# A retention, expert and SoLU kernel on one core: decay table by transposes, last tile's rows turned by DRAM, last scaling on two engines

## The chip, the core and the metric

The kernel runs on one core of a Trainium2 chip. A core has a matrix engine (TensorE, PE here) that reads SBUF and writes PSUM, three engines for elementwise work (VectorE, DVE; ScalarE, ACT; GpSimd, POOL), a sync engine (SyncE, SP) that here issues most transfers, and DMA queues that move data between DRAM and SBUF. Each engine takes its instructions in the order of the program and waits on semaphores for the others. PEld is PE's loading of the stationary operand. The metric is the time of one execution on the device in microseconds; the median of three runs is given.

## What is computed

Three stages, each in float32, on 1536 tokens of 512 numbers (2 batches, 8 heads of 64, 768 steps):

```python
gamma = 1.0 - 2.0 ** (-5.0 - np.arange(H))          # one decay a head
for t in range(S):                                   # retention
    state = gamma * state + outer(k[:, :, t], v[:, :, t])
    y[:, :, t] = (1 / sqrt(D)) * q[:, :, t] @ state
# experts: the two best of 8 by noisy logits, softmax over the two
h = np.maximum(x[mask] @ w1[e], 0.0)
out[mask] += top2_w[mask, k, None] * (h @ w2[e])
# SoLU block: 512 -> 1024 -> 512
h = x @ w_in
solu = h * softmax(h)
ln = (solu - mean(solu)) / sqrt(var(solu) + 1e-6) * g_ln
return ln @ w_out
```

## The kernel before

**Stages.** The tokens are 12 tiles of 128 (`NT = 12`; tile i is chunk i // 2 of batch i % 2). First, attention runs tile by tile in chunks of 128 steps: scores by head (`scores`, L430), masked on DVE (L434), multiplied with the scaled values (`y_out`, L447), scaled by a decay table `decT` while they leave PSUM (L450), and a state per batch (`kv`, L458). Then the tokens of each expert are gathered from DRAM, and eight experts run two products each. Last, the 12 tiles go through the SoLU block. Most products are made of three: each operand is split into a high part (rounded by ACT) and the rest (subtracted by DVE), and high*high, high*low and low*high are added up, so one product of the last stage (`out_mm`, L959) is 24 instructions: 16 with the high part of the rows, then 8 with the low part.

**Order.** The order is the order of the code (`tc.manual_schedule()`): each engine gets its instructions as the functions are called, and tile pools with a few buffers each add the waits.

**The start.** `scale_v(0)` (DVE, L417), `scores(0)`, then `dec_t(0)`: for each of the 8 heads PE multiplies a column of the loaded decay, broadcast to 64 columns, with the identity (L302), which leaves the decay of each head along the free axis on 64 partitions. ACT copies that from PSUM (L304). `kv(0)`, `y_out(0)`, `scores(1)` follow. 34 small products (L269) stand ahead of all.

**The last stage.** The loop over i (L1226 to L1257) works on several tiles at once. In turn i it takes the rows of tile i that came back from DRAM (`z_parts`), scales and stores tile i - 1 (`store_out`), makes the scale of tile i + 1, and lets PE do the input product of tile i + 2 in two halves of 512 columns (`h_in`, 12 instructions each, L866), with the transposes of tile i + 3 between them (`x2_t`). Then come the row maximum (`solu_max`), exponential and normalization (`solu`) of tile i + 2, the turning of its rows, and PE's product of tile i.

**Turning rows.** The product needs the 1024 numbers of a token along partitions. `z_turn` (tiles 1 to 10) does it off PE: DVE transposes 32x32 blocks (L935), SP issues four writes to DRAM (L938) and one read back with the blocks in place (L940); two turns of the loop later `z_parts` rounds what came back to the high part on ACT (L948), and DVE subtracts (L950). `z_t` (tiles 0 and 11) does it with 8 transposes on PE (L920), from whose PSUM ACT and DVE make the two parts (L922, L925). The last tile's product is made in two halves of 256 columns, each scaled by ACT (L965) and stored; the last store is issued by ACT's own queue.

The launch is one program; the block behind `tc.If(full == 1)` does not run with these inputs. `out` is written by the stores of L966 alone.

Of the kernel before, what the change touches and what calls it, by code (L numbers as in the profile page):

```python
# [8 lines left out]
F32 = mybir.dt.float32  # L9
# [6 lines left out]
AF = mybir.ActivationFunctionType  # L16
# [28 lines left out]
def retnet_moe_solu(ctx, tc, qT, kT, k, v, w_gate, w_noise, noise, w1, w2, w_in, w_out, g_ln,  # L45
                    decay, out, dbg=None):
    nc = tc.nc
    B, NC, _, H, D = v.shape
    HP = H // 2
    S = NC * 128  # L50
    NT = B * NC
    E = w1.shape[0]
    DM = H * D
# [19 lines left out]
    def bank(tag, shape=(128, 512)):  # L73
        pool, n = psum[tag]
        return pool.tile(list(shape), F32, tag=tag, name=tag, bufs=n)
# [67 lines left out]
    def row0(i):  # L143
        c, b = order[i]
        return b * S + c * 128
# [145 lines left out]
    def dec_t(c):  # L291
        if c >= NC:
            return
        decT[c] = wk.tile([128, HP, 128], F32, tag="decT" if c else "decT0", name="decT", bufs=2 if c else 1)
        if c:
            for hp in range(HP):
                nc.scalar.activation(decT[c][:, hp], decT[0][:, hp], AF.Copy, scale=step[:, c, hp:hp + 1])
            return
        p = bank("c3", (128, HP, 128))
        for h in range(H):  # L300
            r = slice(h % 2 * 64, h % 2 * 64 + 64)
            nc.tensor.matmul(p[r, h // 2, :], dec[:, 1, c, h:h + 1].to_broadcast([128, D]), ident, start=True, stop=True,  # L302
                             skip_group_check=True)
        nc.scalar.activation(decT[c], p, AF.Copy)  # L304

    def dec_steps():
# [547 lines left out]
    def h_in(i, s):  # L854
        if i >= NT:
            return
        if s == 0:
            PH[i] = bank(f"d{i % 2}", (128, 2, 512))
        hi, lo = X2T[i]
        n = 0  # L860
        for d in range(KD):
            c = slice(d * 128, (d + 1) * 128)
            f = slice(s * 512, s * 512 + 512)
            wh, wl = unit_t[8 * E + d]
            for x, w in ((hi, wh), (hi, wl), (lo, wh)):
                nc.tensor.matmul(PH[i][:, s, :], x[:, c], w[:, 0, f], start=(n == 0), stop=(n == 3 * KD - 1))  # L866
                n += 1

    def row_max(pool, ph):
        t = pool.tile([128, 16], F32, tag="st", name="st", bufs=3)  # L870
        nc.vector.reduce_max(t[:, 0:1], ph, axis=AX.X)
        nc.vector.tensor_scalar_mul(t[:, 0:1], t[:, 0:1], -1.0)
        return t
# [27 lines left out]
    def solu_max(i):  # L901
        if i >= NT:
            return
        ST[i] = row_max(m2, PH[i].rearrange("p a f -> p (a f)"))
# [38 lines left out]
    def z_parts(i):  # L943
        hi = m2.tile([128, KF, 4, 32], F32R, tag="zh", name="zh")
        lo = m2.tile([128, KF, 4, 32], F32R, tag="zl", name="zl")
        t = ZD.pop(i).rearrange("p a k j -> p k a j")
        for k in (slice(0, KF // 2), slice(KF // 2, KF)) if i == 1 else (slice(0, KF),):
            nc.scalar.activation(hi[:, k], t[:, k], AF.Copy)  # L948
        ZT[i] = tuple(x.rearrange("p k a j -> p (k a j)") for x in (hi, lo))
        return lambda: nc.vector.tensor_sub(lo, t, hi)  # L950

    OUT = {}

    def out_mm(i, c=slice(0, DM)):
        hi, lo = ZT[i]
        p = bank("b")[:, c]
        terms = [(z, f, n) for z, ns in ((hi, (0, 1)), (lo, (0,))) for f in range(KF) for n in ns]
        for m, (z, f, n) in enumerate(terms):
            nc.tensor.matmul(p, z[:, f * 128:(f + 1) * 128], unit_t[8 * E + 4 + f // 2][n][:, f % 2, c],  # L959
                             start=(m == 0), stop=(m == len(terms) - 1))  # L960
        OUT[i] = p

    def store_out(i, c=slice(0, DM)):
        o = m2.tile([128, DM], F32, tag="o", name="o", bufs=3)
        nc.scalar.activation(o[:, c], OUT.pop(i), AF.Copy, scale=RS[i])  # L965
        (nc.scalar if c.stop == DM and c.start else nc.sync).dma_start(out[row0(i):row0(i) + 128, c], o[:, c])  # L966


    ep = ex_ctx.enter_context(tc.tile_pool(name="ep", bufs=1, reuse_waits="tile"))
# [253 lines left out]
    feed(n_units, n_units)  # L1223
    h_in(1, 1)

    for i in range(NT):  # L1226
        gather(i + 5)
        low = None
        if i == 0:
            z_t(0, lambda: solu_max(1))  # L1230
            solu(1)
            z_turn(1)
            RS[0] = RS[0]()
        else:
            if i < NT - 1:
                low = z_parts(i)
            store_out(i - 1)
        if i + 1 < NT:
            RS[i + 1] = RS[i + 1]()
        h_in(i + 2, 0)  # L1240
        if low:
            low()
        x2_t(i + 3)
        mix(i + 4)
        h_in(i + 2, 1)
        solu_max(i + 2)
        solu(i + 2)
        if i + 2 < NT - 1:
            z_turn(i + 2)
        if i == NT - 2:  # L1250
            z_t(i + 1)
        if i < NT - 1:
            out_mm(i)
        else:
            for c in (slice(0, DM // 2), slice(DM // 2, DM)):
                out_mm(i, c)
                store_out(i, c)  # L1257
# [135 lines left out]
```

## Time and profile before

| | |
|---|---|
| median of 3 runs | 514.53 us (514.43 to 514.7) |
| the profiled execution | 515.7 us, its span 513.9 us |
| PE busy | 506.6 us (99% of the span), 3068 instructions |
| PEld, weight loads | 463.9 us (90%) |
| DVE busy | 364.6 us (71%) |
| ACT busy | 233.2 us (45%) |
| POOL busy | 106.3 us (21%) |
| DMA | 111.92 MB, mean 218 GB/s |
| granted TensorE clock | 0.998 of full |

The span runs from the first to the last instruction of the profiled execution. Busy times of engines overlap each other. Times in rows are microseconds from the span's start, and a duration stands behind each start; "idle before" is the time that the engine stood before the row, with what released it. Rows of PE can overlap by a fraction of a microsecond, since products are pipelined; the chain of waits shows the same work without overlap.

### The profile page before, as it was taken

The page shows a single profiled execution, that of the slowest core. Times are in us where ns is not written, and L with a number is a line of the kernel's source. Part 1 is how long each engine was busy: PE and PEld are TensorE (multiplying, and loading weights), DVE is VectorE, ACT ScalarE, POOL GpSimd, SP SyncE. Part 2 cuts the span into 40 slices and gives each one's busy share as a digit, 9 for nine tenths or more (in the row PEclk, how much of TensorE's full clock was granted, in tenths as well). Part 3 has the DMA queues.
Part 4 walks back from the last instruction along what each step waited for, and adds up shares of the span by engine and source line. Part 5 has one row for each costly group of instructions (what it writes and reads, how often), then busy time and mean ns, then how long its engine had stood idle before and what let it go on. Part 6 is the DMA issues. An engine that isn't in the chain of part 4 may idle for free.

```text
span 513.9 us, 8633 instructions
## 1 busy us (share of the span) xinstructions
PE 506.6 (99%) x3068; PEld 463.9 (90%) x3068; DVE 364.6 (71%) x731; ACT 233.2 (45%) x440; POOL 106.3 (21%) x209
## 2 busy tenths in 40 slices
PE   9999999999999999999999999999999999999996
PEld 8898898989999999999999999998878888888885
DVE  4668778756876886877778778799277767666650
ACT  2578734443353443344435443545354644444431
POOL 4124100513002104004003000002244336311120
PEclk9999999999999999999999999999999999999999
DMA  8989531797978988979899968568553565643341
GB/s 259 347 319 368 208 103 42 243 348 266 328 225 230 294 248 203 352 199 283 296 239 324 288 200 237 198 172 222 160 190 106 166 184 149 206 134 103 102 123 47
DMA packets 71857, 111.92 MB, mean 218 GB/s; under 512 B 9760, under 2 KB 37152, under 8 KB 71808
## 3 DMA queue, kind: packets, MB, share of 16 engines
q1 hardware_dynamic: 65952, 96.54, 61.5%
q0 software_dynamic: 4368, 14.29, 8.9%
q10 hardware_dynamic: 1488, 0.48, 0.4%
q8 instruction: 26, 0.43, 0.4%
q14 instruction: 23, 0.19, 0.1%
HBM read 83.50 MB, written 27.79 MB: 217 GB/s over the span
## 4 chain that ended last, share of the span: by engine, by line
PE 90%; issue 5%; DMA 2%; DVE 2%; POOL 1%; ACT 0%; POOLq 0%; ACTq 0%; DVEq 0%
PE c L1077 23%; PE b L959 13%; PE b L729 12%; PE a L729 12%; PE d L866 11%; PE c L1200 3%; PE xr L480 3%; PE s L430 3%; PE c L447 2%; PE c L458 2%; PE c L443 2%; DMA xr<-xd,rows_r 2%; PE a L844 1%; PE c L269 1%; DVE wl L197 0%
## 5 line engine op out<-in xcount | busy, mean ns | idle before, releaser
L201 DVE TENSOR_TENSOR wl<-wr,wh 128x1024 fp32r<-128x1024 f32 x64 | 76.7, 1219 | 13.5 <-ACT wh L200 13.5
L1077 PE MATMUL c<-hh,wh 128*128 128x448 f32 (+5 forms) x224 | 79.1, 353 | 0.0
L1077 PE MATMUL c<-hl,wh 128*128 128x448 f32 (+5 forms) x224 | 78.9, 352 | 0.0
L1077 PE MATMUL c<-hh,wl 128*128 128x448 f32 (+5 forms) x224 | 78.8, 352 | 0.0
L200 ACT ACTIVATE wh<-wr 128x1024 fp32r<-128x1024 f32 x68 | 69.4, 1049 | 8.5 <-DMA wr<-in_moe_w_dram 8.5
L729 PE MATMUL b<-xh,wh 128*128 128x192 f32 (+8 forms) x144 | 47.2, 335 | 0.2 <-ACT xh L644 0.2
L729 PE MATMUL b<-xh,wl 128*128 128x192 f32 (+8 forms) x144 | 46.7, 332 | 0.0
L1077 PEld LDWEIGHTS c<-hh,wl 128*128 128x128 f32 x224 | 42.2, 188 | 1.3
L1077 PEld LDWEIGHTS c<-hh,wh 128*128 128x128 f32 x224 | 42.1, 188 | 1.3
L1077 PEld LDWEIGHTS c<-hl,wh 128*128 128x128 f32 x224 | 42.1, 188 | 1.3
L729 PE MATMUL a<-xh,wh 128*128 128x256 f32 (+7 forms) x128 | 43.1, 341 | 0.0
L729 PE MATMUL a<-xh,wl 128*128 128x256 f32 (+7 forms) x128 | 42.9, 339 | 0.0
L866 PE MATMUL d<-wh,x2h 128*128 128x512 f32 x96 | 38.8, 404 | 0.0
L959 PE MATMUL b<-wh,zh 128*128 128x512 f32 (+1 forms) x104 | 38.4, 375 | 0.0
L959 PE MATMUL b<-wl,zh 128*128 128x512 f32 (+1 forms) x104 | 38.4, 375 | 0.0
L866 PE MATMUL d<-wl,x2h 128*128 128x512 f32 x96 | 37.9, 395 | 0.0
L866 PE MATMUL d<-wh,x2l 128*128 128x512 f32 x96 | 37.8, 394 | 0.0
L1115 POOL COPY pace<-hh 1x1 f32<-1x1 f32 x20 | 9.7, 485 | 135.4 <-ACT hh L733 135.4
L733 ACT ACTIVATE hh<-b 128x192 fp32r<-128x192 f32 (+8 forms) x36 | 17.1, 475 | 43.6 <-PE b L729 40.9
L733 ACT ACTIVATE hh<-a 128x256 fp32r<-128x256 f32 (+7 forms) x32 | 15.9, 496 | 45.8 <-PE a L729 45.8
L1040 ACT ACTIVATE xh<-xt 128x428 fp32r<-128x428 f32 (+5 forms) x24 | 13.0, 540 | 45.1 <-DVE xt L1038 45.1
L1004 POOL DMA_INDIRECT xr<-xd,rows_r x27 | 28.1, 1040 | 25.4 <-DVE rows_r L677 15.9
(258 smaller groups left out, 1091.5 us busy)
## 6 DMA issues: line engine op xcount, KB each, us to landing
wr<-in_moe_w_dram SPq DMA_DIRECT2D x64, 512.0 KB
zd<-zs SPq DMA_DIRECT2D x40, 128.0 KB
zc<-zd SPq DMA_DIRECT2D x10, 512.0 KB
xs<-xr SPq DMA_DIRECT2D x18, 256.0 KB
raw<-in_moe_w_in_dram SPq DMA_DIRECT2D x8, 512.0 KB
raw<-in_moe_w_out_dram SPq DMA_DIRECT2D x8, 512.0 KB
xq<-xs SPq DMA_DIRECT2D x16, 208.0 KB
yg<-yr SPq DMA_DIRECT2D x16, 208.0 KB
```

The source lines that it names most:

```text
L200: nc.scalar.activation(hi, t, AF.Copy)
L201: (nc.gpsimd if u < LEAD else nc.vector).tensor_sub(lo, t, hi)
L430: nc.tensor.matmul(p[:, s, hp, :], KT[i][r, hp, :], QT[i][r, hp, :], start=True, stop=True)
L480: nc.tensor.matmul(t[:, d // 2, at:at + 128 + G2], XT[i][:, d, :], unit[d // 2][:, G2 - G2 * (d % 2):][:, :128 + G2], start=(d % 2 == 0), ...
L729: nc.tensor.matmul(p, w[:, 0, f * 128:(f + 1) * 128], x[:, d, c], start=(n == 0), stop=(n == len(terms) - 1))
L733: nc.scalar.activation(hh[:, f, c], p, AF.Relu)
L866: nc.tensor.matmul(PH[i][:, s, :], x[:, c], w[:, 0, f], start=(n == 0), stop=(n == 3 * KD - 1))
L959: nc.tensor.matmul(p, z[:, f * 128:(f + 1) * 128], unit_t[8 * E + 4 + f // 2][n][:, f % 2, c], start=(m == 0), stop=(m == len(terms) - 1))
L1004: nc.gpsimd.indirect_dma_start(out=t[b], out_offset=None, in_=xd[:], in_offset=bass.IndirectOffsetOnAxis(ap=rows_r[:, e - 1, b:b + 1], axi ...
L1040: nc.scalar.activation(hi, t, AF.Copy)
L1077: nc.tensor.matmul(py[d][:, :CAPS[e]], c, h[:, f, :CAPS[e]], start=(f == 0 and n == 0), stop=(f == KF - 1 and n == 2))
L1200: nc.tensor.matmul(py, h[:, f, c], w[:, f % 2], start=(f == 0 and n == 0), stop=(f == KF - 1 and n == 2))
```

## The change

Four things change in the code.

**The decay table.** `dec_t(0)` first lets DVE copy the eight columns, each spread over 64 columns, to a tile `wide` (128x512, in the ring of the `xT` tiles), and PE then transposes its four 128x128 blocks. ACT's copy from PSUM stays.

**The last tile's rows.** Tile 11 goes through `z_turn` and `z_parts` as the others do; ACT's rounding is in two halves there, as for tile 1. `z_t` is left for tile 0.

**A product begun inside another's place.** `out_mm` takes a part of its 24 instructions. In turn 8 PE does the first 12 of tile 8's product; the other 12 come in turn 9, behind the input product of tile 11. Tile 8 is scaled and stored after the exponential of tile 11. The small tiles `st` get a fourth buffer.

**The last scaling.** Of the last 256 columns DVE scales 128 and ACT 128.

```diff
--- before.py
+++ after.py
@@ -296,11 +296,12 @@
             for hp in range(HP):
                 nc.scalar.activation(decT[c][:, hp], decT[0][:, hp], AF.Copy, scale=step[:, c, hp:hp + 1])
             return
+        wide = wk.tile([128, HP, 128], F32, tag="xT", name="wide", bufs=3)
+        nc.vector.tensor_copy(wide.rearrange("p q (s d) -> p (q s) d", s=2),
+                              dec[:, 1, c, :, None].to_broadcast([128, H, D]))
         p = bank("c3", (128, HP, 128))
-        for h in range(H):
-            r = slice(h % 2 * 64, h % 2 * 64 + 64)
-            nc.tensor.matmul(p[r, h // 2, :], dec[:, 1, c, h:h + 1].to_broadcast([128, D]), ident, start=True, stop=True,
-                             skip_group_check=True)
+        for hp in range(HP):
+            nc.tensor.transpose(p[:, hp, :], wide[:, hp, :], ident)
         nc.scalar.activation(decT[c], p, AF.Copy)
 
     def dec_steps():
@@ -867,7 +868,7 @@
                 n += 1
 
     def row_max(pool, ph):
-        t = pool.tile([128, 16], F32, tag="st", name="st", bufs=3)
+        t = pool.tile([128, 16], F32, tag="st", name="st", bufs=4)
         nc.vector.reduce_max(t[:, 0:1], ph, axis=AX.X)
         nc.vector.tensor_scalar_mul(t[:, 0:1], t[:, 0:1], -1.0)
         return t
@@ -944,26 +945,33 @@
         hi = m2.tile([128, KF, 4, 32], F32R, tag="zh", name="zh")
         lo = m2.tile([128, KF, 4, 32], F32R, tag="zl", name="zl")
         t = ZD.pop(i).rearrange("p a k j -> p k a j")
-        for k in (slice(0, KF // 2), slice(KF // 2, KF)) if i == 1 else (slice(0, KF),):
+        for k in (slice(0, KF // 2), slice(KF // 2, KF)) if i in (1, NT - 1) else (slice(0, KF),):
             nc.scalar.activation(hi[:, k], t[:, k], AF.Copy)
         ZT[i] = tuple(x.rearrange("p k a j -> p (k a j)") for x in (hi, lo))
         return lambda: nc.vector.tensor_sub(lo, t, hi)
 
     OUT = {}
 
-    def out_mm(i, c=slice(0, DM)):
+    def out_mm(i, c=slice(0, DM), part=slice(0, 3 * KF)):
         hi, lo = ZT[i]
-        p = bank("b")[:, c]
+        if not part.start:
+            OUT[i] = bank("b")[:, c]
         terms = [(z, f, n) for z, ns in ((hi, (0, 1)), (lo, (0,))) for f in range(KF) for n in ns]
-        for m, (z, f, n) in enumerate(terms):
-            nc.tensor.matmul(p, z[:, f * 128:(f + 1) * 128], unit_t[8 * E + 4 + f // 2][n][:, f % 2, c],
+        for m, (z, f, n) in list(enumerate(terms))[part]:
+            nc.tensor.matmul(OUT[i], z[:, f * 128:(f + 1) * 128], unit_t[8 * E + 4 + f // 2][n][:, f % 2, c],
                              start=(m == 0), stop=(m == len(terms) - 1))
-        OUT[i] = p
 
     def store_out(i, c=slice(0, DM)):
         o = m2.tile([128, DM], F32, tag="o", name="o", bufs=3)
-        nc.scalar.activation(o[:, c], OUT.pop(i), AF.Copy, scale=RS[i])
-        (nc.scalar if c.stop == DM and c.start else nc.sync).dma_start(out[row0(i):row0(i) + 128, c], o[:, c])
+        p = OUT.pop(i)
+        if c.start and c.stop == DM:
+            m = (c.start + c.stop) // 2
+            nc.vector.tensor_scalar_mul(o[:, m:c.stop], p[:, m - c.start:], RS[i])
+            nc.scalar.activation(o[:, c.start:m], p[:, :m - c.start], AF.Copy, scale=RS[i])
+            nc.scalar.dma_start(out[row0(i):row0(i) + 128, c], o[:, c])
+        else:
+            nc.scalar.activation(o[:, c], p, AF.Copy, scale=RS[i])
+            nc.sync.dma_start(out[row0(i):row0(i) + 128, c], o[:, c])
 
 
     ep = ex_ctx.enter_context(tc.tile_pool(name="ep", bufs=1, reuse_waits="tile"))
@@ -1223,6 +1231,7 @@
     feed(n_units, n_units)
     h_in(1, 1)
 
+    HALF = 12
     for i in range(NT):
         gather(i + 5)
         low = None
@@ -1232,9 +1241,9 @@
             z_turn(1)
             RS[0] = RS[0]()
         else:
-            if i < NT - 1:
-                low = z_parts(i)
-            store_out(i - 1)
+            low = z_parts(i)
+            if i != NT - 3:
+                store_out(i - 1)
         if i + 1 < NT:
             RS[i + 1] = RS[i + 1]()
         h_in(i + 2, 0)
@@ -1243,13 +1252,17 @@
         x2_t(i + 3)
         mix(i + 4)
         h_in(i + 2, 1)
+        if i == NT - 3:
+            out_mm(i - 1, part=slice(HALF, 3 * KF))
         solu_max(i + 2)
         solu(i + 2)
-        if i + 2 < NT - 1:
+        if i == NT - 3:
+            store_out(i - 1)
+        if i + 2 < NT:
             z_turn(i + 2)
-        if i == NT - 2:
-            z_t(i + 1)
-        if i < NT - 1:
+        if i == NT - 4:
+            out_mm(i, part=slice(0, HALF))
+        elif i < NT - 1:
             out_mm(i)
         else:
             for c in (slice(0, DM // 2), slice(DM // 2, DM)):
```

On PE, the start before (`c_285` is the PSUM tile of the decay table, `unit_169` holds the identity):

```order
L430 MATMUL s<-qt,kt 128x128 x8
L302 MATMUL c_285<-unit_169,dec 64x128 x8
L458 MATMUL c_256<-vp,kn 128x128 x4
L447 MATMUL c_313<-pm,vp 64x128 x8
L430 MATMUL s<-qt,kt 128x128 x8
```

and on PE, the same place now:

```order
L431 MATMUL s<-qt,kt 128x128 x8
L304 MATMUL c_287<-unit_169,wide 128x128 x4
L459 MATMUL c_256<-vp,kn 128x128 x4
L448 MATMUL c_311<-pm,vp 64x128 x8
L431 MATMUL s<-qt,kt 128x128 x8
```

The eight products with the decay are replaced by four that read `wide`, at the same place between the first scores and the update of the state.

On DVE, the start now, where `wide` is made (before, the same rows stood there without the copy):

```order
L283 TENSOR_SCALAR causal<-jp 128x128
L285 TENSOR_SCALAR before<-jp 128x128
L418 TENSOR_TENSOR vp<-vt,dec 128x512
L435 TENSOR_TENSOR pm<-s,causal 128x512 x2
L300 COPY wide<-dec 128x512
L451 TENSOR_TENSOR xT<-c_311,decT 128x512
```

The copy stands behind the two masked scores, which read the PSUM tile `s` of the first scores.

On PE, near the end, before: the end of the input product of tile 11 (`d1_5382`) and what follows (`b_5419` is the product of tile 9):

```order
L866 MATMUL d1_5382<-wh_4184,x2h_5308 128x512
L866 MATMUL d1_5382<-wl_4185,x2h_5308 128x512
L866 MATMUL d1_5382<-wh_4184,x2l_5309 128x512
L959 MATMUL b_5419<-wh_4188,zh_5369 128x512
L959 MATMUL b_5419<-wl_4189,zh_5369 128x512
```

and on PE, the same place now (`d1_5365` is the input product of tile 11, `b_5342` the product of tile 8, `b_5426` that of tile 9):

```order
L867 MATMUL d1_5365<-wl_4183,x2h_5306 128x512
L867 MATMUL d1_5365<-wh_4182,x2l_5307 128x512
L961 MATMUL b_5342<-wh_4423,zh_5274 128x512
L961 MATMUL b_5342<-wl_4424,zh_5274 128x512
L961 MATMUL b_5342<-wh_4423,zh_5274 128x512
L961 MATMUL b_5342<-wl_4424,zh_5274 128x512
L961 MATMUL b_5342<-wh_4186,zl_5275 128x512 x2
L961 MATMUL b_5342<-wh_4194,zl_5275 128x512 x2
L961 MATMUL b_5342<-wh_4417,zl_5275 128x512 x2
L961 MATMUL b_5342<-wh_4423,zl_5275 128x512 x2
L961 MATMUL b_5426<-wh_4186,zh_5355 128x512
```

The second half of tile 8's product, 4 instructions with the high part and 8 with the low part, has moved behind the input product of tile 11 and ahead of tile 9's.

On ACT, the last rows before, with the semaphores that each waits for (`zh<-a` are the last tile's rows from PE's transposes):

```order
L879 ACTIVATE ee,st<-d_5382,st 128x1024 [waits DVE_49,PE_49,Activation_49]
L948 ACTIVATE zh<-zc 128x1024 [waits DMAHW5_49]
L965 ACTIVATE o<-b,st 128x512 [waits DMAHW2_49,PE_49,Pool_49]
L890 ACTIVATE ee,st<-z 128x1024 [waits DVE_49]
L922 ACTIVATE zh<-a 128x512 [waits PE_49] x2
L965 ACTIVATE o<-b,st 128x512 [waits DMAHW0_49,PE_49,Pool_49]
L965 ACTIVATE o<-b,st 128x256 [waits DMAHW6_49,PE_49,Pool_49]
L965 ACTIVATE o<-b,st 128x256 [waits DMAHW7_49,PE_49,Activation_49]
L966 DMA out_dram<-o 128x256 [waits DMAHW2_49,Activation_49]
```

and on ACT, the last rows now:

```order
L880 ACTIVATE ee,st<-d_5365,st 128x1024 [waits DVE_49,PE_49,Activation_49]
L973 ACTIVATE o<-b,st 128x512 [waits DMAHW4_49,PE_49,Pool_49]
L949 ACTIVATE zh<-zc 128x1024 [waits DMAHW5_49]
L973 ACTIVATE o<-b,st 128x512 [waits DMAHW2_49,PE_49,Pool_49]
L891 ACTIVATE ee,st<-z 128x1024 [waits DVE_49]
L949 ACTIVATE zh<-zc 128x512 [waits DMAHW3_49,Activation_49]
L949 ACTIVATE zh<-zc 128x512
L973 ACTIVATE o<-b,st 128x512 [waits DMAHW0_49,PE_49,Pool_49]
L973 ACTIVATE o<-b,st 128x256 [waits PE_49,DMAHW6_49,Activation_49,Pool_49]
L970 ACTIVATE o<-b,st 128x128 [waits DMAHW4_49,DVE_49,Activation_49]
L971 DMA out_dram<-o 128x256 [waits DMAHW7_49,Activation_49]
```

The scaling of tile 8 stands behind the exponential of tile 11, the last tile's rows come from DRAM (`zc`), and the last 128 columns wait for DVE in place of PE.

## Rows read from the trace of the kernel before

**Rows 1.** The page: busy time of each engine, its share, its instructions.

```profile
PE 506.6 (99%) x3068; PEld 463.9 (90%) x3068; DVE 364.6 (71%) x731; ACT 233.2 (45%) x440; POOL 106.3 (21%) x209
```

**Rows 2.** Waits of PE, longest that it has: us in total, times, longest.

```profile
PE a L1034 <- DMA xr<-xd,rows_r: 0.8, 1, 0.8
```

**Rows 3.** Chain of waits, the start: start us, us, engine, tile, line.

```profile
1.05 3.81 PE c L269 x34
4.86 1.81 PE s L430 x16
6.68 1.02 PE c L302 x16
7.70 1.09 PE c L458 x8
...
9.81 1.09 PE s L430 x16
```

**Rows 4.** Timeline of DVE, the start: start us, us, what [idle before].

```profile
6.73 1.29 DVE L434 TENSOR_TENSOR pm<-s,causal 128x512 f32<-128x512 f32 x2 [0.55 <-PE s L430]
...
9.93 0.69 DVE L450 TENSOR_TENSOR xT<-c,decT 128x512 f32<-128x512 f32 x1 [1.91 <-PE c L447]
```

**Rows 5.** Groups of DVE by form, 0 to 30 us: busy us, mean ns.

```profile
L367 DVE CAST col<-col 128x128 f16<-128x128 f32 x1 | 0.2, 221 | 0.0
```

**Rows 6.** Groups of DVE by form, 380 us to the end.

```profile
L950 DVE TENSOR_TENSOR zl<-zc,zh 128x1024 fp32r<-128x1024 f32 x10 | 12.0, 1195 | 2.9 <-ACT zh L948 2.9
L885 DVE TENSOR_SCALAR z<-ee,st 128x1024 f32<-128x1024 f32 x12 | 9.8, 813 | 0.4
```

**Rows 7.** Groups of ACT by form, 380 us to the end.

```profile
L965 ACT ACTIVATE o<-b,st 128x512 f32<-128x512 f32 x11 | 7.5, 682 | 10.4 <-issue 5.7 <-PE b L959 4.7
...
L948 ACT ACTIVATE zh<-zc 128x512 fp32r<-128x512 f32 x2 | 1.2, 625 | 2.9 <-DMA zc<-zd 2.9
L965 ACT ACTIVATE o<-b,st 128x256 f32<-128x256 f32 x2 | 0.9, 474 | 4.5 <-PE b L959 4.5
```

**Rows 8.** Chain of waits, the end.

```profile
480.69 5.50 PE b L959 x24
...
491.77 5.50 PE b L959 x24
497.27 1.06 PE a L920 x8
498.33 11.16 PE b L959 x72
...
509.56 0.47 ACT o L965
```

**Rows 9.** Timeline of DVE, SP's queue and ACT: tile 10's way through DRAM.

```profile
486.13 1.25 DVE L935 STREAM_TRANSPOSE zs<-z 128x1024 f32<-128x1024 f32 x1
487.41 1.77 SPq L938 DMA_DIRECT2D zd<-zs  x4
491.11 0.34 SPq L940 DMA_DIRECT2D zc<-zd  x1
495.09 1.07 ACT L948 ACTIVATE zh<-zc 128x1024 fp32r<-128x1024 f32 x1 [0.49 <-DMA zc<-zd]
```

**Rows 10.** Timeline of SP's queue and ACT: two other tiles' way.

```profile
391.53 1.78 SPq L938 DMA_DIRECT2D zd<-zs  x4
398.81 1.15 ACT L948 ACTIVATE zh<-zc 128x512 fp32r<-128x512 f32 x2 [2.88 <-DMA zc<-zd]
399.81 1.75 SPq L938 DMA_DIRECT2D zd<-zs  x4
407.90 1.06 ACT L948 ACTIVATE zh<-zc 128x1024 fp32r<-128x1024 f32 x1 [1.80 <-DMA zc<-zd]
```

**Rows 11.** Stretches: us, busy us of five engines (x), granted clock, DMA share, GB/s.

```profile
105.60:106.50 0.90, 0.10 (x2) 0.06 (x1) 0.00 (x0) 0.00 (x0) 0.00 (x0) 1.00 1.03 412
511.60:511.80 0.20, 0.00 (x0) 0.00 (x0) 0.00 (x0) 0.00 (x0) 0.00 (x0) 0.50 0.00 0
```

## The prediction

> **What bounds the kernel now.** I read the page first: TensorE (PE) is busy for 506.6 us of a span of 513.9 us [rows 1]. Then the waits by engine: in all that time PE waits for anything measurable only a handful of times, the longest being 0.8 us for the gathered rows of the second expert [rows 2]. So a microsecond of PE work removed is worth a microsecond, and a microsecond in which PE stands is lost, unless that one wait gives it back. Other engines matter only where PE waits for them. I then read the two places that the change touches: the first microseconds, in the chain of waits and the timeline [rows 3, 4], and the last forty, in the same two views [rows 8, 9]. In both, PE rows follow each other without a gap: whatever the change puts between them shows in the time.
>
> The rows come from one execution of 515.7 us with a span of 513.9 us; the median of the three timed runs is 514.53 us. I work out a difference against the span's own rows and add it to the median.
>
> **The start: the decay table.** Before, PE goes from the first scores at 6.68 to the eight products with the broadcast decay (L302), which take 1.02 and end at 7.70, when the update of the state (L458) begins [rows 3]. These products wait for nothing but the decay and the identity, long there. Now there are four transposes of `wide`, and `wide` is a copy by VectorE (DVE). DVE takes its instructions in the order written, and the order places the copy behind the two masked scores (L434). These cannot start before PE has finished the scores: they run from 6.73 for 1.29, to 8.02 [rows 4]. So PE has nothing to do from 6.68 until the copy is there, and the state update, the first output and the next scores are queued behind the transposes on PE.
>
> The copy itself, 128x512 f32 with a repeated column as its source, is in no row. The nearest are a one-input 128x128 cast of 0.22 [rows 5] and a one-input 128x1024 scaling of 0.81 [rows 6]; on the line between them 512 columns take 0.47. The ends: 0.22, as if it cost no more than 128 columns, and 0.69, which a two-input 128x512 takes [rows 4]. I take 0.47, since a copy has one input as those two rows have. The hand-over from DVE I take as 0.03, which stands between the end of a DVE transpose (486.13 + 1.25) and the first copy issued after it (487.41) [rows 9]. Four transposes are half of the eight that take 1.06 at the end [rows 8], 0.53. So they end at 8.02 + 0.47 + 0.03 + 0.53 = 9.05 instead of 7.70: **+1.35**, from +1.10 to +1.57. That PE does 0.49 less work is already in it. DVE's copy delays nothing on DVE: the next instruction there (L450) sat idle for 1.91, waiting for PE [rows 4]. ScalarE's copy of the table is later too, but is wanted first by L450, which also waits for L447 behind the transposes on PE. What comes after is PE work row on row, so nothing there absorbs the delay; the single place that could is a rival below.
>
> [...]
>
> **The end: the last tile by DRAM.** Removed are the eight transposes of the last tile on PE: 1.06, in a row between the products of the last but two and last but one tiles [rows 8]. The second half of tile 8's product (12 of 24 products, 2.75 of 5.50) is moved behind the last input product; the same work, so PE's sum does not change. What is new is the trip through DRAM. Call T the time when PE has finished a tile's input product. For tile 10, T is 480.69, where the next product begins [rows 8]; DVE's transposed rows are done at 487.38, the first of the four writes is issued at 487.41, the read back at 491.11, and ScalarE (ACT) starts on the rows that have landed at 495.09, having idled 0.49 for them [rows 9]. So the trip is 7.68 from the first write's issue and the rows are there at T + 14.40.
>
> For the last tile DVE does the same work in the same order after T; ahead of it on SP's queue only the store of tile 8 is new, whose product is done at T + 2.75 and whose scaling takes ACT 0.68 [rows 7], so that it is issued well before the first write at T + 6.72. Nothing on the four writes or on the read is moved past something late. ACT is free at T + 14.40, converts the first half in 0.62 [rows 7], and PE can begin the last product at T + 14.40 + 0.62 + 0.03 = T + 15.05. What PE has till then is 12 + 24 + 24 products: 2.75 + 5.50 + 5.50 = 13.75. It waits for 15.05 - 13.75 = 1.30. Against the 1.06 saved: **+0.24**. The other trips that ACT waited for were 398.81 - 391.53 = 7.28 and 407.90 - 399.81 = 8.09 [rows 10]; with these it is -0.16 and +0.65. I take 7.68, the trip at the same place with the same store beside it. The low parts come in time, just: both halves are converted at T + 15.55 (the pair took 1.15 [rows 10]), the subtraction takes 1.20 [rows 6], so T + 16.78; PE reaches them after 16 products of 256 columns, each (11.16 - 5.50) / 48 = 0.118 [rows 8], at T + 16.94. Tile 10's own conversion and subtraction keep their times and are wanted a microsecond later; the later store of tile 8 frees its PSUM bank well before the product of tile 10 asks for it. The fourth `st` buffer costs nothing.
>
> **The last scaling.** Before, ACT scales 128x256 in 0.47 [rows 7, 8] after PE's last product. Now DVE scales 128 columns and ACT 128, but the order shows ACT's half waiting for DVE, not for PE, and no other DVE work is left to wait for: the two run one after the other. ACT's 128 columns: 0.474 less half of what 256 columns more cost (0.682 - 0.474) gives 0.37 [rows 7]. DVE's: 128 columns from SBUF took 0.22 [rows 5], 512 from PSUM 0.69 [rows 4]; I take 0.28, nearer to the first, and 0.40 as the high end. 0.28 + 0.03 + 0.37 = 0.68 instead of 0.47: **+0.21**, at most +0.43; were the two at once after all, 0.37, so -0.10.
>
> [...]
>
> **Sum.** 1.35 + 0.24 + 0.21 = +1.80, which is 516.3 us. All low ends give 1.10 - 0.16 - 0.10 = +0.84 (515.4), all high ends 1.57 + 0.65 + 0.43 = +2.65 (517.2).
>
> **Rivals.**
> The first ends on the other side: the trip is short. If the last tile's rows are there by T + 13.10, PE never stops, the whole 1.06 is kept, and the sum is 1.35 - 1.06 + 0.21 = +0.50: 515.0, not slower. It decides below a trip of 7.68 - 0.77 = 6.9, where the sum passes 1.03. For it: nothing reads weights any more then. Against it: that was so for tile 10 too, and no trip shown was under 7.28. Chance 0.09.
> The second: the delay of the start is taken up by the wait for the gathered rows, if these come at a time of their own. At most the 0.8 of that wait [rows 2]: +1.0, 515.5. Against it: the gather's rows come out of the attention outputs and of lists that PE makes in its turn, so they are later by as much. Chance 0.07.
> The third: the clock. [...] PE now stands for 1.84 in the start (6.68 to 8.52) and 1.30 near the end. [...] If it falls, PE needs time to get its rate back: it has products from 1.05 on, yet the first scores, from 4.86, took 1.81 and the next 1.09 for the same 16 rows [rows 3]. So the full rate came some 4 to 5.5 us after the first product, and half of that, 2.0 to 2.8, would be lost on top: 518.3 to 519.1, 518.7 in the middle. Chance 0.15.
> The fourth: it does what it seems meant to, the copy not in PE's way, the trip and the scaling hidden: -0.49 - 1.06 - 0.10 = -1.65, 512.9. The order of DVE speaks against it. Chance 0.04.
>
> **How the numbers follow.** 0.65 for the forecast, 516.3 with a range of its own of 515.4 to 517.2. A measurement of this kernel tells about 0.2% from no change, 1.03 us: 513.5 to 515.56. Slower: the forecast but for its lowest edge, and the clock, 0.78. Same: the short trip, the gather and that edge, 0.18. Faster: the fourth, 0.04. The range that holds 8 in 10 takes the forecast and the two rivals below it (0.81), from 515.0. Above it reaches to 517.6, beyond the 517.2 of the high ends, since the length of the last trip is known from three trips only.
>
> **What would show it.** In the changed profile: PE idle of some 1.8 before the four transposes, released by DVE's copy; the update of the state starting near 9.05; the chain at the end going through the read back from DRAM and ACT's first half, with PE idle of about 1.3 before the last product; DVE's 128x128 and ACT's 128x128 one after the other; the granted clock at 1.00 after both stops. Wrong it would be if the copy ran beside PE work, if a PE wait near 105 us shrank by as much as the start lost, or if the trip took under 7 us.

## The result, and the profile after

The changed kernel takes 518.66 us (median of 6 runs, 517.15 to 519.91) against 514.62 beside it: a ratio of 1.0077, interval 1.0061 to 1.0093. It is slower by 4.0 us; the forecast said slower by 1.8. Beside the experiments the changed kernel came out at 518.12 and 519.11, with the kernel before at 514.25 and 514.57. The times of all 18 executions fall into two groups by the mean granted TensorE clock: at 0.999 nine of 517.15 to 518.52, at 0.989 to 0.996 nine of 518.66 to 522.41. Three executions of 619 to 836 us (one of the kernel before, one of e7_all_mended, one of e12_end_wait), at a mean granted clock of 0.56 to 0.75, stand in no ratio below, and the two medians that count one of them, 514.05 and 517.1, are 513.85 and 516.98 without it.

The profile after is of the shortest execution (517.15, span 515.4). PE does less, as meant (against [rows 1]):

```profile
PE 504.2 (98%) x3048; PEld 462.2 (90%) x3048; DVE 366.6 (71%) x733; ACT 233.5 (45%) x440; POOL 107.7 (21%) x209
```

What it saves it waits: PE's waits by what they were for (total, times, longest), where before the longest was the 0.8 for the gathered rows [rows 2]. (A wait of 1.1 ahead of PE's very first product stands in both profiles; [rows 2] leaves it out.)

```profile
PE c L304 <- DVE wide L300: 1.8, 1, 1.8
PE b L961 <- ACT zh L949: 1.6, 1, 1.6
```

**The start**, in the chain of waits (start, duration, what) and in DVE's timeline, which answer to [rows 3, 4]:

```profile
4.87 1.38 PE s L431 x16
6.27 1.29 DVE pm L435 x2
7.55 0.34 DVE wide L300
7.90 0.14 issue
8.03 0.63 PE c L304 x4
8.66 0.89 PE c L459 x8
```

```profile
7.47 0.41 DVE L300 COPY wide<-dec 128x512 f32<-128x512 f32 x1
10.70 0.69 DVE L451 TENSOR_TENSOR xT<-c,decT 128x512 f32<-128x512 f32 x1 [2.81 <-PE c L448]
```

PE stands from the end of the scores until the masks and the copy are done. The copy took 0.41 (0.42 in e9_act_alone below), where the forecast had 0.47.

**The end**, in the chain of waits, against [rows 8, 9], and the last two scalings in the timeline (in brackets the idle before and its releaser):

```profile
495.58 0.32 SPq L939
...
496.91 2.33 DMA zd<-zs
...
499.37 3.98 DMA zc<-zd
...
503.43 0.64 ACT zh L949
504.11 6.03 PE b L961 x48
```

```profile
510.22 0.35 DVE L969 TENSOR_SCALAR o<-b,st 128x128 f32<-128x128 f32 x1 [4.39 <-PE b L961]
510.66 0.37 ACT L970 ACTIVATE o<-b,st 128x128 f32<-128x128 f32 x1 [2.76 <-DVE o L969]
```

The way through DRAM ends the wait ahead of the last product. ACT waits for DVE: 0.81 from the start of the first scaling to the end of the second, instead of 0.47.

The last product is 6.03 of the chain, where the same 48 instructions were 11.16 - 5.50 = 5.66 in [rows 8]. Part of that is how the chain counts: it has no overlap, and behind a stop there is nothing to overlap with. So here are the first and the last row of the 48 in the timeline of PE (start, duration), in the profile before, after, and in e10_low_later below, where no stop stands ahead of them:

```profile
503.67 0.28 PE L959 MATMUL b<-wh,zh 128*128 128x256 f32 x1
...
508.38 1.10 PE L959 MATMUL b<-wh,zl 128*128 128x256 f32 x8
```

```profile
504.11 0.39 PE L961 MATMUL b<-wh,zh 128*128 128x256 f32 x1 [1.63 <-ACT zh L949]
...
509.01 1.12 PE L961 MATMUL b<-wh,zl 128*128 128x256 f32 x8
```

```profile
500.95 0.39 PE L961 MATMUL b<-wh,zh 128*128 128x256 f32 x1
...
505.85 1.12 PE L961 MATMUL b<-wh,zl 128*128 128x256 f32 x8
```

From first start to last end that is 5.81 before, 6.02 after and 6.02 without the stop.

### The profile page after: what moved, and what is told of

The parts are those of the page before. It is cut to its first block, busy times and chain, and to the rows that moved or that the text cites. A ratio compares the mean times of both kernels' runs of the same rounds, so it can differ in the third digit from the quotient of the medians.

```text
span 515.4 us, 8617 instructions
## 1 busy us (share of the span) xinstructions
PE 504.2 (98%) x3048; PEld 462.2 (90%) x3048; DVE 366.6 (71%) x733; ACT 233.5 (45%) x440; POOL 107.7 (21%) x209
## 4 chain that ended last, share of the span: by engine, by line
PE 85%; issue 5%; DMA 4%; DVE 3%; ACT 1%; POOL 1%; SPq 0%; ACTq 0%; POOLq 0%; DVEq 0%
PE c L1085 23%; PE a L730 12%; PE b L730 12%; PE d L867 10%; PE b L961 10%; PE c L1208 3%; PE xr L481 3%; PE s L431 3%; PE c L448 2%; PE c L459 2%; PE c L444 2%; DMA xr<-xd,rows_r 2%; DMA zc<-zd 1%; PE a L845 1%; DMA zd<-zs 1%
```

## The experiments

Times beside a run are those of the kernel before on the same chip.

**The profile that the forecast rests on.** The kernel before again, without an edit, three times.

> The kernel before unchanged, for its profile: the one the forecast rests on took 515.70 us, the median of the timed runs 514.3 to 514.6. Theory BASE (that profile was of a long execution): this one takes 514.0 to 514.8, and the 1.2 us between stand in rows: the first scores 1.1 to 1.4 us instead of 1.81, and the wait for the second expert's rows under 0.5 instead of 0.8. Theory PROFILE (being profiled costs the kernel before 1.2 us): 515.7 again, with the same rows.

> As the other profile of the kernel before. Theory BASE: 514.0 to 514.8, the first scores and the wait for the second expert's rows shorter than in the profile that the forecast rests on. Theory PROFILE: 515.7 with the same rows.

> As the other profiles of the kernel before. Theory BASE: 514.0 to 514.8, with the first scores and the wait for the second expert's rows shorter. Theory PROFILE: 515.7 with the same rows.

They took 514.83, 514.29 and 514.21. Rows of the third, in the chain:

```profile
4.86 1.22 PE s L430 x16
6.08 1.02 PE c L302 x16
...
8.19 1.02 PE c L447 x16
...
497.03 10.96 PE b L959 x72
```

Theory BASE holds, though two of the first scores are above its 1.1 to 1.4. They took 1.54, 1.50 and 1.22 instead of 1.81, the wait for the gathered rows was 0.3 in the first and not listed in the other two, instead of 0.8, and the chain's last 72 products took 10.96 instead of 11.16. The rows ahead of the prediction come from an execution that was long by some 1.2 us; the usual one has nothing for a delay of the start to be absorbed in.

**Each part alone.** The start in the kernel before (e1_start_only), and, the same edit the other way round, the changed kernel with the old start (e2_tail_only):

```diff
-for h in range(H):
-    nc.tensor.matmul(p[r, h // 2, :], dec[:, 1, c, h:h + 1].to_broadcast([128, D]), ident, ..)
+nc.vector.tensor_copy(wide.rearrange(..), dec[:, 1, c, :, None].to_broadcast([128, H, D]))
+for hp in range(HP):
+    nc.tensor.transpose(p[:, hp, :], wide[:, hp, :], ident)
```

> The kernel before with the decay table by copy and transposes alone; the end is as before. Clock theory: PE's stop of some 1.8 us in the start keeps PE at its lower rate for longer in most executions. Then this alone gives most of the loss and its scatter: 516.5 to 518.5 us. Trip theory: the excess over the forecast comes from the last tile's way through DRAM. Then this gives only the stop itself, about +1.0 to +1.4: 515.6 to 516.0, with no more scatter than the kernel before.

> The changed kernel with the decay table made as before; the last tile by DRAM, the moved half product and the shared scaling stay. Clock theory: only the wait of 1.5 us before the last product and the two scalings one after the other remain, about +0.4 to +0.9 net of the transposes saved: 515.0 to 515.5, little scatter. Trip theory: most of the loss stays, 517 to 518, scattered.

The start alone: 516.65 against 514.29 (1.0052, 1.0032 to 1.0073). The tail alone: 518.45 (1.0078, 1.0054 to 1.0101). Neither theory had it: the first time lies in the clock theory's range and the second above both. The loss isn't at the start alone, and the two parts sum to more than the whole. In the tail's profile (519.93) the wait, the chain, and the stretches with PE's busy time and, third from the right, the granted clock:

```profile
PE b L960 <- ACT zh L948: 3.1, 1, 3.1
```

```profile
495.81 3.77 DMA zd<-zs
...
504.50 8.71 PE b L960 x48
```

```profile
501.00:503.00 2.00, 0.38 (x2) 0.00 (x0) 0.00 (x0) 0.00 (x0) 0.00 (x0) 1.00 0.90 242
...
504.00:510.00 6.00, 5.50 (x25) 5.50 (x26) 1.23 (x1) 1.55 (x3) 0.00 (x0) 0.50 0.11 44
```

The fourth write landed in 3.77 instead of 2.33, PE stood for 3.1, the granted clock fell to 0.50, and the last product took 8.71. The mean clock was 0.992 to 0.995 in all six executions, so it fell in each; where, only the profiled one shows. What the late write met is in the trace's DMA packets. At 497 to 498 us the DMA queues have this row (queue, kind, packets, MB, share of the engines):

```profile
q8 instruction: 1, 0.02, 6.0%
```

It is a load of instructions, 16 KB, from 497.15 to 498.11. The writes' packets had all begun by 497.73, but for the last 18, the first of which began at 498.10. None of the other eleven profiles with this way has such a load between its four writes. Which engine's instructions it brought, and why just here, isn't shown.

**PE kept busy in the stop at the start.** Products of ones, whose sums nobody reads, stand ahead of the transposes.

```diff
+busy = bank("c2")
+for n in range(30):
+    nc.tensor.matmul(busy[:, :128], ones, ones, start=True, stop=True)
 for hp in range(HP):
```

> The changed kernel with 30 products of the constant ones (into a PSUM bank not yet in use, result unused) put on PE ahead of the four transposes, so that PE works while DVE makes the copy. Clock theory: the stop is still there for the useful work, but PE is busy, so only the forecast's terms remain: 515.9 to 516.5, little scatter. Trip theory: nothing changes, about 518.5, scattered.

517.18 against 514.29 (1.0062, 1.0043 to 1.0082), and the mean clock 0.998 to 1.000 in all six executions, where the changed kernel had 0.996 or less in nine of 18. So the stop at the start is one of the places where the clock falls, worth about a microsecond on the median. The time is between the two theories' (515.9 to 516.5, about 518.5): the clock is a part of the loss and not the whole.

**The copy ahead of the masks**, behind the scaling of v:

```diff
 scale_v(0)
+wide = ..; nc.vector.tensor_copy(wide, ..)
 scores(0)
```

> The changed kernel with the copy placed ahead of the masked scores on DVE, where DVE stood idle, so that PE does not wait for it. Clock theory, and the start's own cost: PE saves about 0.5 and does not stop; with the end's +0.4 to +0.9 that is 514.5 to 515.1, little scatter. Trip theory: 516.5 to 517.5, scattered.

516.3 against 514.29 (1.0049, 1.0032 to 1.0066); the stop shrank to 0.9. The clock theory's 514.5 to 515.1 was missed, since the loss at the end stays; the trip theory's 516.5 to 517.5 was missed by 0.2.

**The changed kernel again, then its end.** First no edit.

> The changed kernel unchanged, as the measure for the other three. Both theories: about 518.5 us and a wide spread over its executions (517 to 520), PE's wait ahead of the last product 1.6 to 3.1 us. Theory END CLOCK: in the executions near 517 the granted clock stays at 1.00 through the last product (about 6.0 us long); in the longer ones it falls to 0.50 and the last product takes 7 to 9 us. Theory TRIP: the spread is that of the transposes' way through DRAM alone, and the last product is 6.0 us long in every execution.

518.12 (517.93 to 520.28). In its profile (518.15) tile 11's input product ends at T = 490.03, the last product begins at 505.26 after a wait of 1.7. Its two theories speak of the longer executions, and this is none; the one long execution of this kernel with a profile, a2_after below (519.56), has its last product at 6.03 and its fall of the clock at the start, against theory END CLOCK. Then the whole of tile 8's product behind that input product; and, separately, 24 products of ones in the wait:

```diff
# e5_no_wait
-out_mm(i - 1, part=slice(HALF, 3 * KF))
+out_mm(i - 1)
...
-if i == NT - 4:
-    out_mm(i, part=slice(0, HALF))
-elif i < NT - 1:
+if i < NT - 1 and i != NT - 4:
     out_mm(i)
-else:
+elif i == NT - 1:
# e6_fill_tail
+busy = bank("a")
+for n in range(24):
+    nc.tensor.matmul(busy[:, :128], ones, ones, start=True, stop=True)
 for c in (slice(0, DM // 2), slice(DM // 2, DM)):
     out_mm(i, c)
```

> All 24 products of tile 8's output stand behind tile 11's h_in, so PE has work until the rows through DRAM are there (11.2 us of products more than a half of them gives; the rows came 7.85 us after the first write was issued). PE doesn't wait ahead of the last product. Theory END CLOCK: what a stop at the end costs, wait and slower product, is gone: 515.5 to 516.3 us and a spread of 0.6 us or less, the rest over the kernel before being the start (about 1) and the last scaling (0.34). Theory TRIP: only the wait is gone, 1.6 us of the 518.5, so about 516.9, with the same time for the last product. Rival START (the rate of the first 10 us makes the loss): 518, as the changed kernel.

> 24 products of ones, about 1.4 us of work whose sum nobody reads, stand on PE ahead of the last product, in the stop; when the last rows come is unchanged. Theory END CLOCK: the stop left over is 0.2 to 0.5 us, the granted clock stays at 1.00 through the last product, the time is 516.8 to 517.4 with a spread of 0.8 us or less. Theory TRIP: the wait's end doesn't move, so the time is that of the changed kernel, 518.5, and so is its spread.

e5_no_wait: 516.98 against 514.25 (1.0050), near theory TRIP's 516.9, but that theory had no wait left and PE still waits 1.0. e6_fill_tail: 517.92 (1.0070), 0.2 less than the changed kernel, the last product at 504.07 as late as ever and 6.01 from first start to last end, the mean clock 0.997 to 1.000. Filling the stop gained next to nothing here, where the clock didn't fall: the wait itself is the price, as theory TRIP has it, though its 518.5 was 0.6 too high. Why a wait was left is seen with the next run.

**All parts mended:** e5_no_wait, the copy first of all on DVE, the last scaling by ACT alone.

```diff
+wide = ..; nc.vector.tensor_copy(wide, ..)
 scale_v(0)
...
-nc.vector.tensor_scalar_mul(o[:, m:c.stop], ..)
-nc.scalar.activation(o[:, c.start:m], ..)
+nc.scalar.activation(o[:, c], p, AF.Copy, scale=RS[i])
```

> As the run without a wait, and besides the spread columns are made first of all on VectorE, ahead of the scaling of v, and ScalarE alone does the last scaling (0.47 us against the 0.81 of two engines one after the other). Theory END CLOCK: start 0.5 to 0.9 us shorter than the changed kernel's, no wait at the end, scaling 0.34 less: 514.0 to 515.2 us, at or a little under the kernel before, small spread. Theory TRIP: 515.3 to 516. Rival START: above 517.

514.05 against 514.25 (0.9995, 0.9986 to 1.0005): what the three parts lost is gone. DVE's timeline at the end, and the wait:

```profile
486.24 1.18 DVE L951 TENSOR_TENSOR zl<-zc,zh 128x1024 fp32r<-128x1024 f32 x1
487.34 1.21 DVE L872 TENSOR_REDUCE st<-d 128x1 f32<-128x1024 f32 x1
```

```profile
PE b L961 <- ACT zh L949: 1.0, 1, 1.0
```

PE has finished the input product at 485.20, but DVE begins its row maximum (L872) 2.1 later: the subtraction for tile 9's low parts (L951) stands ahead. In the changed kernel DVE was free only 0.6 before T, so moving PE's work bought that 0.6 and no more.

**That subtraction behind the row maximum**, beside ACT's exponential:

```diff
-if low:
+if low and i != NT - 3:
     low()
...
 solu_max(i + 2)
+if i == NT - 3:
+    low()
```

> The run with all parts mended still waited 1.0 us ahead of the last product, since VectorE began tile 11's row maximum 2.1 us after PE had the input product: the subtraction for tile 9's low parts (1.18 us) stood ahead of it. Here that subtraction stands behind the row maximum, beside ScalarE's exponential. Theory END WAIT: rows there at T + 15.2, PE busy to T + 16.5, no wait before the last product, so 1.0 us less than the run with all parts mended: 513.0 us, 0.2% under the kernel before, its spread about 1 us or less. Theory START (what is lost is lost in the first 10 us): no change from 514.05.

512.98 against 514.37: 0.9974, 0.9966 to 0.9983. This beats both kernels. No wait of the products is left at the end, and the first output (L445) starts at 8.15, here and in e7_all_mended, against 8.51 on average in six profiles with the old start:

```profile
6.48 0.63 PE c L301 x4
7.11 1.04 PE c L456 x8
8.15 1.02 PE c L445 x16
...
484.77 22.21 PE b L961 x120
```

```profile
485.82 1.18 DVE L872 TENSOR_REDUCE st<-d 128x1 f32<-128x1024 f32 x1
...
487.12 1.23 DVE L951 TENSOR_TENSOR zl<-zc,zh 128x1024 fp32r<-128x1024 f32 x1
```

**What the sharing costs, and the end wait by itself.** The changed kernel again; without the sharing (edit as in e7_all_mended); the kernel before with the sharing alone; and the changed kernel with only the orders of e5_no_wait and e10_low_later.

> The changed kernel unchanged, the measure for the other three on their chip: about 518.1 to 518.7 us, PE's wait ahead of the last product 1.6 to 1.8 us or, with a late write, 3; the last store lands 2.3 to 2.8 us after its issue.

> The changed kernel with the last 256 columns scaled by ScalarE alone. Theory SHARE (the sharing also makes the last store late): 0.34 us from the scaling (0.47 instead of 0.81) and 0.5 to 0.8 from the store, which lands in 1.8: 0.8 to 1.1 us less than the changed kernel beside it, about 517.2. Theory SERIAL (the sharing costs its rows only): 0.34 less, about 517.9, the store landing in 2.3 to 2.8 as before.

> The kernel before with the sharing of the last scaling alone. Theory SHARE: 0.8 to 1.1 us more than the kernel before, about 515.3, the last store landing in 2.3 to 2.8. Theory SERIAL: 0.34 more, about 514.7, the store landing in 1.8.

> The changed kernel with the whole of tile 8's output product behind tile 11's input product and the subtraction for tile 9's low parts behind tile 11's row maximum, so that the rows through DRAM come before PE has done its work; start and last scaling as changed. Theory END WAIT: no wait ahead of the last product (1.65 less), which takes 5.7 us and not 6.0 (0.3 less), and no fall of the clock there: 1.9 to 2.4 us less than the changed kernel beside it, about 516.0. Theory START (the rate lost in the first 10 us makes most of the missing time): 1.0 less at most, about 517.3.

Against 514.57: the changed kernel 519.11 (1.0098, 1.0070 to 1.0126), without the sharing 517.71 (1.0057, 1.0040 to 1.0075), the sharing alone 515.54 (1.0015, 1.0002 to 1.0029), without the end wait 517.1 (1.0047, 1.0031 to 1.0064). Theory SHARE holds in its kind: the sharing costs 1.0 alone, where the two engines in a row explain 0.34. In the changed kernel leaving it out gains 1.4, above the 0.8 to 1.1 expected; that kernel's executions lie as far apart as that. The rest is the last store. Its row (size, median us from issue to landing) of the changed kernel, and of the kernel before:

```profile
out_dram<-o ACTq DMA_DIRECT2D x1, 128.0 KB, 2.6
```

```profile
out_dram<-o ACTq DMA_DIRECT2D x1, 128.0 KB, 1.8
```

In all ten profiles with the sharing it took 2.3 to 2.8, in the seven without, where the view gives it, 1.8. The trace's DMA packets show why the same 128 KB land later. In the profile after, at 511.8 to 512.2 us, the DMA queues have this row:

```profile
q14 instruction: 1, 0.01, 10.9%
```

It is a load of instructions, 8 KB, from 511.94 to 512.64. Of the store's 128 packets 120 have begun by 1.38 us after ACT's end, as in a store without the sharing; the other eight begin one after the other from 512.64 on. All ten profiles with the sharing have such a load, begun 0.9 to 1.3 after ACT's end, and six to eight late packets that begin when it ends; the eight without have neither. DVE's last branch stands 0.14 ahead of ACT's end with the sharing and 5.4 to 9.3 ahead of it without. ACT's own branch is followed by such a load after 1.1; that the load in question is DVE's is read from these times and not tested by a run of its own.

Theory END WAIT holds too: 2.0 less, with 1.9 to 2.4 expected. Its 0.3 for a faster last product did not come: the 48 took 6.01 from first start to last end.

The profile of e9_act_alone (517.84) shows the clock fall at the start: DVE's timeline, the chain, and two stretches with the granted clock third from the right.

```profile
5.71 0.69 DVE L418 TENSOR_TENSOR vp<-vt,dec 128x512 f32<-128x512 f32 x1 [3.54 <-DMA dec<-in_decay_dram]
...
7.52 0.42 DVE L300 COPY wide<-dec 128x512 f32<-128x512 f32 x1
```

```profile
8.08 1.09 PE c L304 x4
9.17 1.71 PE c L459 x8
```

```profile
7.50:8.25 0.75, 0.17 (x1) 0.20 (x2) 0.43 (x2) 0.00 (x0) 0.58 (x4) 0.82 1.04 377
8.25:10.50 2.25, 2.25 (x12) 2.25 (x11) 0.00 (x0) 0.60 (x1) 0.14 (x2) 0.50 1.05 391
```

Here the scores were done at 6.02, but DVE had the decay only at 5.68 and first scaled v. PE stood for 2.1, the clock fell to 0.50, and transposes and state update took 1.09 and 1.71 instead of 0.63 and 0.89. Eight profiles have this start with nothing in the stop: five with stops of 1.8 to 1.9 kept 1.00, three with 2.0 to 2.1 (e5_no_wait, a2_after, e9_act_alone) lost it. The length isn't shown to be what decides: the three are also the ones whose clock had risen first, at 4.0 to 4.6 us by the trace's records, against 5.3 to 6.7 in the five.

## Why the prediction was right and wrong

The direction, and the path of each of the three losses, came as forecast. The time was above the range (517.6), since every term was too small. The steps that failed are the size of the end's term (0.24, measured about 1.05), the last store, taken as unchanged (it landed 0.5 to 1.0 later), and the clock at the start, left out of the sum at a chance of 0.15 (it fell in three profiles of eight).

- **The start, +1.35.** The step holds at equal scores: with 1.39 for them the old start (e2_tail_only) reaches the state update at 7.28, with 1.38 the changed one at 8.66, +1.38, and +1.18 at the first output, as the update was shorter. The copy was shorter too (0.41 for 0.47), the hand-over longer (0.14 for 0.03). What failed is the weight of the third rival, 0.15. Over the eight profiles the first output starts at 10.30 on average (9.55 to 10.98), with the old start at 8.51 (six profiles, 8.19 to 8.79): +1.79, most of the difference being the clock in three of them. Timed alone the start costs 2.4; some 0.6 of that no row places.
- **The wait at the end, 1.30.** Measured 1.6 to 1.9, and 3.1 where a write was late. From the first write's issue to ACT's start it was 7.85 (495.58 to 503.43; 7.68 taken), and in e8_after_again the last product began at T + 15.23 (15.05 taken), PE's own work ending at T + 13.5 (13.75 taken). So a trip some 0.2 longer and work some 0.2 shorter made the wait longer. The trips were within the bounds, 7.48 to 8.09, but for the one with the late write, 9.34.
- **The last product, taken at its old length.** The forecast has no term for it. In the chain its 48 instructions are 6.03 behind the stop, against 5.66 before and 10.96 - 5.50 = 5.46 in the three later profiles: 0.36 to 0.56 more. They are not slower because of the stop. From first start to last end they take 6.00 to 6.02 in all eleven profiles with these rows at a granted clock of 1.00, with the stop, with the stop filled (e6_fill_tail) and with none (e10_low_later, e12_end_wait); with the old rows it is 5.81 in three profiles and 5.60 in three. A stop adds that the first of them cannot overlap the one ahead, 0.15 in e10_low_later. Why they take longer with rows that came through DRAM, and why the old ones take two values, is open.
- **The last scaling, +0.21.** Serial as the order showed, +0.34, since DVE's half took 0.35 and not 0.28 and its hand-over 0.09 and not 0.03. The two at once, at -0.10, did not come: in all ten profiles with the sharing ACT starts 0.43 to 0.44 after the start of DVE's 0.35 to 0.36, and what keeps them apart is the wait in the order. Its high end is added up wrong: 0.40 + 0.03 + 0.37 - 0.47 is +0.33 and not +0.43, so all high ends give 517.1. The step that failed: it ended at ACT's last row, and the store behind it was taken as unchanged. That landed 0.5 to 1.0 later, held up by a load of instructions; the part alone costs 1.0. Behind the landing the changed kernel ends 0.36 sooner (1.72 for 2.08 in every profile), which no term had either.
- **The sum.** 1.79 for the start, 1.65 - 1.05 + (0.36 to 0.56), about 1.05, for the end, and 1.0 for the sharing less 0.36 behind the landing make 3.5, against 3.9 to 4.5 measured. At the end the clock may add to this in some executions; no profile of the changed kernel shows it there.
- **Rivals.** The short trip and the change doing as meant did not come. The gather took up part of the delay in the profiled execution (last attention rows +0.71, at 106 us +0.18), but only because the wait was 0.8 in the profile before; it is 0.3 or less in the later profiles of that kernel. The clock rival's time, 518.3 to 519.1, holds the median, which is luck in part: for half the executions, at a mean clock of 0.999, the other terms alone made 517.15 to 518.52. Its price at the start was 1.3 and not 2.0 to 2.8; at the end, once and in another kernel (e2_tail_only), 8.71 - 6.03 = 2.7. The half in it is the 0.50 of [rows 11]; the four profiles with a fall under PE's work (e2_tail_only, e5_no_wait, a2_after, e9_act_alone) show 0.50 again. Its reading of the first scores agrees with the estimate in the last section.

## What to carry to other kernels

Here an edit that removed PE work but let PE stand paid for the stop (1.8 at the start, 1.6 at the end) and, in three profiles of eight, for the clock at the start (1.3); so first find what the engine ahead of the stop has in its queue (here masks ahead of a copy, a subtraction ahead of a row maximum) and reorder that. Follow the last result to its landing in DRAM, not to the last engine's row (here 2.6 behind its issue instead of 1.8), and look among the DMA packets for what else moved then. Compare a group of products by its first start and last end where a stop stands ahead of it in one kernel only. And profile the kernel before more than once: here one execution's rows lay 1.2 us off the median (515.7 for 514.53).

## What was not expected of the hardware

- The granted clock fell to 0.50 in stops of PE of 2.0 to 2.1 us at the start (e5_no_wait, a2_after, e9_act_alone) and stayed at 1.00 after stops of 1.8 to 1.9 there and 1.6 to 1.9 at the end. But behind PE's last product it stayed at 1.00 for 2.0 us in the profile before (509.48 to 511.51) and for 3.7 us in the profile after (510.13 to 513.88), so the length of a stop alone does not decide. What else does isn't shown; the executions of this one kernel fall into two groups, at a mean clock of 0.999 and of 0.989 to 0.996.
- A load of instructions held up data. With an 8 KB load in its time the last store of 128 KB landed in 2.3 to 2.8 us instead of 1.8 (ten profiles with, eight without); with a 16 KB load in its time a write of 128 KB landed in 3.77 instead of 2.33 (once). In the profile after the load ends and the last eight packets of the store begin at 512.64.
- The first scores, the same 16 rows, took 1.10 to 2.01 us from one execution to the next, and a lower clock ahead of them would explain it. The views print 1.00 there, but the trace's first record of the granted clock, at 1.00, begins only at 3.9 to 6.7 us, and before it there is none. Where it begins by 4.86 the scores took 1.10, at 5.09 they took 1.22, at 6.34 1.81, at 6.71 2.01. An estimate from these rows, half the rate up to the record (the 0.50 above) and the full rate behind it, meets all 18 profiles within 0.07.
